# Zeroed pad columns, a later load and a new order for the head of a block kernel

## The chip, the cores and the metric

The kernel runs on one core of a Trainium2 chip. The metric is the device time of one execution in microseconds (us); a run gives several executions, and their median is compared. The engines of the core are TensorE (PE, with its weight loads PEld), VectorE (DVE), ScalarE (ACT), GpSimd (POOL) and SyncE (SP, which here issues DMAs).

## The reference

One token block with adaptive layer norm: the vector c makes six modulation rows, an attention with a sliding window of 256 follows (16 heads of 28), and then a gated MLP whose gate mixes along the sequence. x is 2048 x 448; everything is bfloat16.

```
mod = (silu(c) @ w_mod).reshape(1, 6, 1, 448)      # w_mod: 448 x 2688
sa, ca, ga, sb, cb, gb = the six rows of mod
h = layernorm(x) * (1 + ca) + sa
x = x + ga * attention(h, wqkv, wo)                # keys within 256 before the query
h = layernorm(x) * (1 + cb) + sb
z = gelu(h @ w_in); z1, z2 = halves of z; z2 = layernorm(z2)
x = x + gb * ((z1 * (w_sp @ z2 + b_sp)) @ w_out)
```

## The kernel before, in words

The kernel is written as a list of operations, each with its dependencies. The string ORDER fixes, in one sequence over all engines, in which order they run: a word such as `158.a` or `50.p.0` is the number of an operation, its engine (p PE, a ACT, v DVE, g POOL, s SP) and, where it takes a buffer, which one. Each engine runs its operations in this order and never out of order. `Sched.order` reads the string, `waits` puts a semaphore wait only where an operation's dependency isn't known to be done, `emit` writes the instructions. An operation that waits therefore holds everything behind it on its engine.

The sequence is cut into 16 tiles of 128 rows and four blocks of 512. The work around the change is that of the first block, in the first 20 us:

- Loads, all on SP in this order: x of tiles 0 to 3 (ops 1, 2), the first 896 columns of w_mod in four row chunks kc (ops 4 to 7, `t_wmA`), the q and k columns of wqkv in chunks (ops 8 to 10; chunk 3 is op 3 on ACT's queue), wv (11, 12), x of tiles 4 to 7 (13), the other 1792 columns of w_mod (14, 15, `t_wmB`), x of tiles 8 to 11 (16).
- c is turned into a column by PE (op 41) and put through silu by ACT in two pieces (ops 42 and 43, `t_sc`). DVE zeroes the padding rows of the fourth chunk of w_mod (23, `t_p2`) and of c's column (22, 25).
- The statistics of tiles 0 to 3: bn_stats and bn_aggr on DVE (L581, L584), the reciprocal root on POOL (L586, L587), xn on DVE (L594), transposes on PE (L625; ops 150, 152, 154, 156).
- The modulation of the first norm: for each chunk kc PE makes eight columns of 128 (L537 to L541; ops 50 to 53, `t_mA`), and DVE adds up the four chunks into modT (op 54, L543). D is 448, so the last of the eight columns holds only 64; before the change it is first written with zeros by a product with the zero tile wz and then its lower half with a product of 64 columns.
- hT: the transposed xn leaves PSUM with scale and shift from modT, one operation for each of four channels ch (ops 157 to 160, in the order ch 3, 0, 1, 2; L635 on ACT, L636 on DVE). Each waits for op 54 and for all four transposes.
- WQK: the q and k weights of each chunk are copied from wq_st into a padded layout (ops 133 to 136; L573 on ACT, L574 on DVE or POOL).
- PE then makes q and k of the block, eight groups of four products (L646), evicted to qT and KT (L654 on ACT, L655 on DVE). Attention starts on those (L855, L881, L842).
- Fillers (L549) are products on wz whose result nobody reads.
- The rows for ga, gb, sb, cb come from a later product of PE with the other columns of w_mod (op 119, `t_rows`, L556), which needs sc_rep (op 48, L531), a copy of c's column repeated 32 times.
- Ops 44 to 47 zero the tile QBD, 27 the padding of wv, 36 writes ones into Vaug, 38 and 39 build the mask.

After the first 20 us the order is the same in both kernels.

Of the kernel before, what the change touches and what calls it, by code (L numbers as in the profile page):

```python
# [23 lines left out]
191.p.0 178.p 163.p 44.g 173.p 179.p 166.p.2 180.a 186.p.1 167.p 174.p 182.p 217.v 175.a 168.p 169.p 215.v 164.p 170.a 187.p 192.p 219.v 188.p 165.a  # L24
189.p 213.v 183.p 190.a 374.p.0 216.v 220.v 184.p 214.v 218.v 375.a.0 193.p 221.g 185.v 196.p.1 222.g 194.p 197.p 195.v 198.p 199.p 201.p.6 225.g
200.v 210.s 227.g 226.g.0 17.s 202.a 380.p.0 228.v.1 381.a.1 223.g 212.s 229.g 224.v.2 119.p.0 30.g 18.s 230.v.3 376.v 211.s 231.p.1 120.a 399.p.0
232.v 121.s 234.p.0 400.a.2 233.v 209.s 203.p.6 235.v 19.s 401.a 205.p.1 236.v 123.s 265.v 204.a 406.p.0 206.v 239.p.0 407.a.3 267.v 378.v 251.p.1
# [239 lines left out]
def bass_adaLN_cond__sliding_block__mixer_gmlp__prompt_kernel(  # L267
# [56 lines left out]
    sc_sb, _, _ = alloc("sc_sb", [128, DC], BF16)  # L324
# [31 lines left out]
    wmod, _, wmod_bytes = alloc("wmod", [128, DC, 6 * D], BF16, at=z2_off)  # L356
# [69 lines left out]
    t_wmA = [chunk("d_wmA", "sp", wmod, w_mod, kc, slice(0, 2 * D), -98.95 + 0.001 * kc, LAND_M[kc], 0.23) for kc in range(DC)]  # L426
# [12 lines left out]
    t_wmB = load2("d_wmB", "sp", 1.4, wmod, slice(2 * D, 6 * D), w_mod, slice(2 * D, 6 * D), (), -94.0)  # L439
# [13 lines left out]
    def pool(dur, fn, deps=(), prio=-90.0):  # L453
        return add({"pool": (dur, fn)}, deps, prio)
# [37 lines left out]
    t_p2 = [dve(1.2, lambda e: e.memset(wmod[64:128, 3, :], 0.0), prio=-98.0)]  # L492
# [29 lines left out]
    t_sc = [  # L522
        act(0.25, lambda e: e.activation(sc_sb[:, 0:3], ps[:, hC.slot[0], 0:3], ACT.Silu), [t_cT, t_p1], -90.0, table="silu"),
        act(0.25, lambda e: e.activation(sc_sb[0:64, 3:4], ps[0:64, hC.slot[0], 3:4], ACT.Silu), [t_cT, t_p1], -90.0, table="silu"),
    ]
# [7 lines left out]
    t_wz = dve(0.08, lambda e: e.memset(wz[:], 0.0), prio=-99.9)  # L533
    hA = Hold(bM)
    t_mA = []
    for kc in range(DC):
        fs = [lambda e, v=v, ch=ch, kc=kc, n=n: e.matmul(  # L537
            ps[:, hA.slot[0], 8 * kc + n:8 * kc + n + 1], lhsT=wmod[:, kc, v * D + ch * 128:v * D + ch * 128 + 128], rhs=sc_sb[:, kc:kc + 1],
            start=True, stop=True) for n, (v, ch) in enumerate((v, ch) for v in (0, 1) for ch in range(DC))][:7]
        fs += [lambda e, kc=kc: e.matmul(ps[:, hA.slot[0], 8 * kc + 7:8 * kc + 8], lhsT=wz[:], rhs=wz[:, 0:1], start=True, stop=True),  # L540
               lambda e, kc=kc: e.matmul(ps[0:64, hA.slot[0], 8 * kc + 7:8 * kc + 8], lhsT=wmod[:, kc, 2 * D - 64:2 * D], rhs=sc_sb[:, kc:kc + 1], start=True, stop=True)]  # L541
        t_mA.append(pe(0.23, fs, [t_wmA[kc], t_sc, t_p2, t_wz] + t_mA[-1:], -60.0 + 0.1 * kc, [] if kc else [hA]))
    t_modA = [dve(0.16, lambda e: e.tensor_reduce(modT[:, 0:8], ps[:, hA.slot[0], 0:32].rearrange("p (k n) -> p n k", k=4), mybir.AxisListType.X, ALU.add), [t_mA], -59.0)]  # L543
    hA.until += t_modA

    def warm(n, dur, times, cols):
# [11 lines left out]
        start=(kc == 0), stop=(kc == DC - 1), tile_position=(0, 32 * i)) for kc in range(DC) for i, v in enumerate((2, 5, 3, 4))],  # L558
# [127 lines left out]
    for tb in range(1, NB4):  # L686
        v = 40.0 * tb - 50.0
# [24 lines left out]
        for cp in range(0 if tb >= PET else 2):  # L712
# [6 lines left out]
            for k in range(2):  # L719
                ch = 2 * cp + k  # L720
# [353 lines left out]
    for tb in range(NB4):  # L1074
# [16 lines left out]
        for i in range(4):  # L1091
# [102 lines left out]
```

## Time and profile before

| | |
|---|---|
| median of 3 runs | 277.41 us (276.78 to 278.3) |
| profiled execution, its own time | 278.0 us |
| its span in the profile | 276.3 us, 7324 instructions |
| busy PE, PEld | 265.5 (96%), 140.1 (51%) |
| busy DVE, ACT, POOL | 163.4 (59%), 128.5 (47%), 116.8 (42%) |
| largest groups | L1079 PE 97.9 us, L842 ACT 67.2 us, L897 DVE 37.6 us |

The span is the time from the first to the last instruction; the execution's own time has 1.7 us around it. Matmuls are pipelined, so a PE that is busy 96% isn't at its peak. In the timeline a row gives start, length, engine, line, operation, what it writes and reads, a count where rows were merged, and in brackets how long the engine was idle before it and what ended that. In the chain of waits a row gives start, length and what held the chain. A DMA row gives size and time from issue to landing.

### The profile page before, as it was taken

The numbers are of one execution on the slowest core, as the hardware profiler recorded it, in microseconds if no ns is written. First come the engines' busy times: TensorE is split into PE (matmuls) and PEld (weight loads), VectorE is DVE, ScalarE is ACT, GpSimd is POOL, SyncE is SP. The second block draws the span as 40 slices with busy tenths as digits, with TensorE's granted clock in tenths as the row PEclk, the third lists the DMA queues.
The fourth block names the chain that finished last, engine by engine and source line by source line (L and its number), as shares of the span: only waits on it lengthen the run. The fifth ranks groups of instructions, "written<-read, shape, count | busy, mean of one in ns | idle before, by whom it ended". The sixth has DMA issues, their size and how long they took to land.

```text
span 276.3 us, 7324 instructions
## 1 busy us (share of the span) xinstructions
PE 265.5 (96%) x3176; PEld 140.1 (51%) x3201; DVE 163.4 (59%) x359; ACT 128.5 (47%) x152; POOL 116.8 (42%) x192
## 2 busy tenths in 40 slices
PE   7899998999999999999999999999999999999995
PEld 2545465656676575544444444444444444544452
DVE  7668999999999999666899210014021222331453
ACT  7589999989999996847766500000000000000000
POOL 5340856055334894896169110018033352541310
PEclk9999999999999999999999999999999999999999
DMA  7956244253763377668699989300000000010024
GB/s 217 359 149 166 56 78 81 59 96 77 227 89 80 62 111 157 98 133 134 131 164 187 189 194 191 75 0 0 0 0 2 0 0 2 0 33 17 19 67 133
DMA packets 66862, 26.48 MB, mean 96 GB/s; under 512 B 57801, under 2 KB 65742, under 8 KB 66830
## 3 DMA queue, kind: packets, MB, share of 16 engines
q1 hardware_dynamic: 66748, 25.90, 44.1%
q8 instruction: 25, 0.41, 0.7%
q10 hardware_dynamic: 82, 0.12, 0.1%
q14 instruction: 7, 0.06, 0.1%
HBM read 9.47 MB, written 1.84 MB: 41 GB/s over the span
## 4 chain that ended last, share of the span: by engine, by line
PE 75%; ACT 10%; DVE 8%; POOL 2%; issue 2%; DMA 2%
PE ps L1079 35%; PE ps L1096 7%; ACT PW L842 7%; PE ps L1055 6%; PE ps L1034 6%; PE ps L881 4%; PE ps L737 3%; PE ps L924 3%; DVE st_all L581 3%; PE ps L949 3%; PE ps L779 2%; PE ps L890 2%; DMA hT<-xn 2%; PE ps L766 1%; ACT PT L842 1%
## 5 line engine op out<-in xcount | busy, mean ns | idle before, releaser
L842 ACT ACTIVATE PW<-ps 128x2048 bf16<-128x2048 f32 (+1 forms) x56 | 67.2, 1240 | 4.4 <-PE ps L881 2.5
L1083 DVE TENSOR_TENSOR tmpg<-ps,bsp_bc 128x512 bf16<-128x512 f32 x28 | 18.9, 688 | 80.0 <-PE ps L1079 70.2
L1086 POOL TENSOR_TENSOR z1T<-tmpg,z1T 128x512 bf16<-128x512 bf16 x28 | 31.9, 1154 | 80.5 <-DVE tmpg L1083 80.5
L1079 PE MATMUL ps<-wspB,z 128*128 128x512 bf16 x219 | 49.2, 379 | 0.3
L1079 PE MATMUL ps<-wspA,z 128*128 128x512 bf16 x219 | 48.7, 379 | 0.4 <-issue 0.2
L897 DVE TENSOR_TENSOR PT<-PW,mask 128x1024 bf16<-128x1024 bf16 x56 | 37.6, 702 | 0.4 <-ACT PW L842 0.3
L1079 PEld LDWEIGHTS ps<-wspA,z 128*128 128x128 bf16 x224 | 21.8, 98 | 26.6 <-issue 0.4
L1079 PEld LDWEIGHTS ps<-wspB,z 128*128 128x128 bf16 x224 | 21.9, 98 | 26.1
L586 POOL TENSOR_SCALAR ve_all<-mv_all 128x1 f32<-128x1 f32 (+2 forms) x37 | 10.7, 299 | 53.0 <-DVE mv_all L584 52.6
L587 POOL TENSOR_TENSOR rs_all<-ve_all,neghalf 128x1 f32<-128x1 f32 (+2 forms) x37 | 26.2, 720 | 0.9
L924 PE MATMUL ps<-Vaug,PT 128*128 128x29 bf16 x496 | 24.6, 176 | 0.3 <-issue 0.3
L924 PEld LDWEIGHTS ps<-Vaug,PT 128*128 128x128 bf16 x496 | 22.1, 96 | 3.5 <-issue 0.8
L1034 PE MATMUL ps<-w_in,hT 64*128 64x448 bf16 x224 | 22.7, 349 | 0.3 <-POOL hT L974 0.3
L1055 PE MATMUL ps<-hT,w_in 64*128 64x512 bf16 x196 | 22.5, 376 | 0.0
L581 DVE BATCH_NORM_STATS2 st_all<-z 128x6 f32<-128x448 bf16 x32 | 17.9, 600 | 4.7 <-ACT z L1041 4.7
L924 PE MATMUL ps<-Vaug,PW 128*128 128x29 bf16 x224 | 20.6, 175 | 0.0
L1096 PE MATMUL ps<-w_out_g,z1T 128*128 128x448 bf16 x105 | 20.4, 352 | 0.0
L581 DVE BATCH_NORM_STATS2 st_all<-x_sb 128x6 f32<-128x448 bf16 x32 | 19.1, 612 | 0.1
L924 PEld LDWEIGHTS ps<-Vaug,PW 128*128 128x128 bf16 x224 | 17.7, 96 | 2.4
L737 PE MATMUL ps<-hT,WQK 128*128 128x512 bf16 x66 | 17.2, 379 | 1.6 <-issue 0.5
L1041 ACT ACTIVATE z<-ps 128x896 bf16<-128x896 f32 x16 | 14.2, 916 | 8.4 <-PE ps L1034 8.4
L1063 ACT ACTIVATE z1T<-ps 128x512 bf16<-128x512 f32 x28 | 15.0, 610 | 6.2 <-PE ps L1055 6.2
(117 smaller groups left out, 332.7 us busy)
## 6 DMA issues: line engine op xcount, KB each, us to landing
out_dram<-fin SPq DMA_DIRECT2D x15, 112.0 KB, 1.7
x_sb<-in_A_x_dram SPq DMA_DIRECT2D x3, 448.0 KB, 5.6
wmod<-in_w_mod_dram SPq DMA_DIRECT2D x1, 1344.0 KB, 9.2
w_in<-in_B_w_in_dram SPq DMA_DIRECT2D x1, 1344.0 KB, 6.1
QBD<-qT SPq DMA_DIRECT2D x16, 64.0 KB, 2.4
wmod<-in_w_mod_dram SPq DMA_DIRECT2D x4, 224.0 KB, 4.3
w_out_g<-in_B_w_out_dram SPq DMA_DIRECT2D x1, 784.0 KB, 6.3
wq_st<-in_A_wqkv_dram SPq DMA_DIRECT2D x3, 224.0 KB, 4.4
```

Source lines behind the costliest of these rows:

```text
L581: st = [dve(0.62 if True else 0, lambda e, t=t, ci=ci, s=s: e.bn_stats(st_all[:, slot, t, ci, :], s()), deps(t), prio) for ci, s in enumer ...
L587: rs = pool(0.53 + 0.15 * len(tiles), lambda e: e.tensor_tensor(rs_all[:, slot, a:b], ve_all[:, slot, a:b], neghalf[:, 0:b - a], ALU.pow), ...
L737: m = pe(4 * MMS, [lambda e, h=h, g=g, kc=kc, tb=tb: e.matmul(ps[:, h.slot[0], :], lhsT=WQK[:, kc, 4 * g:4 * g + 4, :].rearrange("p a b -> ...
L842: ex = act(xdur, lambda e, out_ap=out_ap, in_ap=in_ap: e.activation(out_ap(), in_ap(), ACT.Exp, scale=SCALE), [s], v - 8.0 + u, takes, tab ...
L897: return dve(0.70, lambda e: e.tensor_tensor(cols(hp.slot[0] * 2048 + 1024 * k, [[256, 4], [128, 2], [1, 128]]), cols(at_w() + 128 + 192 * ...
L924: fns.append(lambda e, hp=hp, hO=hO, hi=hi, bi=bi, kb=kb, hd=hd, nb=nb, a=at[hi][bi], p_of=p_of: e.matmul(ps[:, hO.slot[0], 32 * hd:32 * h ...
L1034: return lambda e, kc, p0, start, stop: e.matmul(ps[:, hs[t % 2].slot[hf], 0:D], lhsT=hT[p0:p0 + 64, kc, t * 128:(t + 1) * 128], rhs=w_in[ ...
L1055: return lambda e, kc, p0, start, stop: e.matmul(ps[:, hs[b // 2].slot[b % 2], :], lhsT=w_in[p0:p0 + 64, kc, ft * 128:(ft + 1) * 128], rhs ...
L1079: m = pe(16 * MMS, [lambda e, h=h, si=si, ft=ft, tb=tb: e.matmul(ps[:, h.slot[0], :], lhsT=z2[:, si, ft * 128:(ft + 1) * 128], rhs=(wspA i ...
L1083: a = dve(0.7, lambda e, h=h, ht=ht, tb=tb: e.tensor_tensor(tmpg[:, ht.slot[0], :], ps[:, h.slot[0], :], bsp_bc[:, tb * 512:(tb + 1) * 512 ...
L1086: u = pool(1.16, lambda e, ht=ht, ft=ft, tb=tb: e.tensor_tensor(z1T[tb][:, ft, :], tmpg[:, ht.slot[0], :], z1T[tb][:, ft, :], ALU.mult), [ ...
L1096: return [lambda e, ft=ft: e.matmul(ps[:, h.slot[0], 0:D], lhsT=z1T[t // 4][:, ft, (t % 4) * 128:(t % 4 + 1) * 128], rhs=w_out_g[:, ft, :] ...
```

## The change

- A new operation (1227, `t_pad`) on POOL zeroes columns 896 to 959 of w_mod in SBUF. The eighth column of products then reads 128 columns like the others, the last 64 of them zeros, so the two special products L540 and L541 are gone. Every group of products waits for the pad.
- Those columns belong to the second load of w_mod, so both of its transfers (`t_wmB`) now wait for all four groups of products.
- The head of ORDER is new: op 25 goes ahead of the aggregates, 43 ahead of the QBD zeroing 46, product groups 50 and 51 ahead of the first transposes; 48 and 27 go from right behind op 54 to behind the hT evictions; 158 moves from ACT to DVE, 133 from DVE to ACT; 159 comes before 160; 39 goes behind the second statistics on POOL. SP's order stays.

The head of ORDER (the rest of the string is only wrapped differently):

```diff
-49.v 20.v 1.s 31.g 0.a 3.a 47.a 21.v 23.v 2.s 4.s 32.g 24.v 40.a 5.s 6.s 33.g 37.g 7.s 139.v 34.g 35.g 29.g 55.p.0 56.p.0 57.p.0 41.p.0 38.g 137.v 8.s
-22.v 140.v 138.v 9.s 143.v 141.g 39.g 10.s 25.v 142.g 145.v 42.a 46.a 11.s 144.v 146.v 149.v.0 12.s 147.g 151.v.1 43.a 58.p.0 59.p.0 60.p.0 61.p.0
-62.p.0 63.p.0 64.p.0 65.p.0 66.p.0 67.p.0 150.p.1.2 148.g 26.v 13.s 50.p.0 152.p 14.s 153.v.2 68.p.0 51.p 155.v.3 69.p.0 52.p 15.s 154.p 53.p 16.s
-156.p 136.a 54.v 48.v 27.v 157.v 158.a 133.v 70.p.0 71.p.0 72.p.0 176.p.3 36.v 161.p.4 160.v 134.a 162.p 171.p.5 159.v 181.p.6 172.p 135.g 177.p 45.a
+49.v 20.v 1.s 31.g 0.a 3.a 47.a 21.v 23.v 2.s 4.s 32.g 24.v 40.a 5.s 6.s 33.g 37.g 7.s 139.v 34.g 35.g 1227.g 29.g 55.p.0 56.p.0 57.p.0 41.p.0 38.g
+137.v 8.s 22.v 25.v 140.v 138.v 9.s 143.v 141.g 10.s 142.g 145.v 42.a 43.a 46.a 11.s 144.v 146.v 149.v.0 12.s 147.g 151.v.1 58.p.0 59.p.0 60.p.0
+61.p.0 62.p.0 63.p.0 64.p.0 65.p.0 66.p.0 67.p.0 50.p.0 51.p 150.p.1.2 148.g 39.g 26.v 13.s 152.p 153.v.2 68.p.0 155.v.3 69.p.0 52.p 154.p 53.p 14.s
+15.s 16.s 156.p 136.a 133.a 54.v 157.v 158.v 70.p.0 71.p.0 72.p.0 176.p.3 36.v 161.p.4 159.v 160.v 134.a 162.p 171.p.5 48.v 27.v 181.p.6 172.p 135.g
```

```diff
     for kc in range(DC):
         fs = [lambda e, v=v, ch=ch, kc=kc, n=n: e.matmul(
             ps[:, hA.slot[0], 8 * kc + n:8 * kc + n + 1], lhsT=wmod[:, kc, v * D + ch * 128:v * D + ch * 128 + 128], rhs=sc_sb[:, kc:kc + 1],
-            start=True, stop=True) for n, (v, ch) in enumerate((v, ch) for v in (0, 1) for ch in range(DC))][:7]
-        fs += [lambda e, kc=kc: e.matmul(ps[:, hA.slot[0], 8 * kc + 7:8 * kc + 8], lhsT=wz[:], rhs=wz[:, 0:1], start=True, stop=True),
-               lambda e, kc=kc: e.matmul(ps[0:64, hA.slot[0], 8 * kc + 7:8 * kc + 8], lhsT=wmod[:, kc, 2 * D - 64:2 * D], rhs=sc_sb[:, kc:kc + 1], start=True, stop=True)]
-        t_mA.append(pe(0.23, fs, [t_wmA[kc], t_sc, t_p2, t_wz] + t_mA[-1:], -60.0 + 0.1 * kc, [] if kc else [hA]))
+            start=True, stop=True) for n, (v, ch) in enumerate((v, ch) for v in (0, 1) for ch in range(DC))]
+        t_mA.append(pe(0.37, fs, [t_wmA[kc], t_sc, t_p2] + t_mA[-1:], -60.0 + 0.1 * kc, [] if kc else [hA]))
...
+    t_pad = pool(0.35, lambda e: e.memset(wmod[:, :, 2 * D:2 * D + 64], 0.0), t_p2[0:1], prio=-97.0)
+    for op in t_mA:
+        op.deps.add(t_pad)
+    for op in t_wmB:
+        op.deps.update(t_mA)
+
     sc.order()
```

More of the change, by code (lines that the diff above doesn't have):

```diff
@@ L24 @@
[L24 to L27, printed above, removed]
@@ new lines @@
+201.p.6 225.g 200.v 210.s 227.g 226.g.0 17.s 202.a 380.p.0 228.v.1 381.a.1 223.g 212.s 229.g 224.v.2 119.p.0 30.g 18.s 230.v.3 376.v 211.s 231.p.1
+120.a 399.p.0 232.v 121.s 234.p.0 400.a.2 233.v 209.s 203.p.6 235.v 19.s 401.a 205.p.1 236.v 123.s 265.v 204.a 406.p.0 206.v 239.p.0 407.a.3 267.v
+378.v 251.p.1 266.v 269.v 408.a 271.v 428.p.0 377.p.0 240.a 379.p 268.v 272.v 426.p.0 270.v 252.v 273.g 243.p.0 274.g 427.a.4.0 402.v 384.v 382.v
+237.p.1 279.g 244.v 280.g.0 383.p 238.v 429.a 434.p.0 275.g 285.s 409.v 247.p.0 435.a.5.1 28.v 325.v 128.g 241.p.1 248.v 321.v 281.g 457.p.0 277.g
@@ new lines @@
+306.v 466.a 126.g 291.p.1 514.a.3.1 461.p.0 468.v 339.s 295.p.0 467.v 292.a 330.v.3 462.p 517.v 296.a 521.p.0 488.v 486.p.0 522.a.4.2 303.p.1 489.v
+469.p 496.v 389.p.0 304.a 526.v 470.p 487.a 542.p.0 471.v 472.v.1 297.p.1 543.a.5.3 390.v 473.s 494.p.0 497.v 490.p.0 491.p 391.v 498.p 337.s 495.a
+518.v 550.p.0 298.v 499.p 551.a.6.4 445.p.0 500.v 340.s 501.v.0 416.p.1 446.v 525.v 515.p.0 338.s 571.p.0 516.a 546.v 293.p.0 572.a.0.0 447.v 392.v
+519.p.0 417.v 393.g 520.p 394.g 502.s 554.v 523.p.0 301.p.1 524.a 395.g 294.v 396.v.0 579.p.0 124.s 302.a 576.v 299.p.0 307.s 580.a.1.1 343.g 418.v
@@ new lines @@
+310.s 448.v 474.p.1 555.v 308.s 344.g 419.v 552.p.0 475.v 527.p 300.a 309.s 528.p 341.g 553.a 600.p.0 529.v 530.v.2 420.g 317.p.1 449.g 601.a.2.2
+397.g 584.v 531.s 503.p.0 450.g 583.v 544.p.0 451.g 547.v 548.p.0 398.s 545.a 608.p.0 342.v 318.a 504.v 573.p.0 549.p 476.v 574.a 556.p 557.p
+609.a.3.3 575.v 345.p.1 477.v 558.v 559.v.1 581.p.0 311.p.0 605.v 560.s 346.a 505.v 629.p.0 582.a 604.v 577.p.0 630.a.4.4 130.s 349.p.1 452.v.1 612.v
+578.p 350.v 610.p.0 585.p 611.a 634.v 637.p.0 312.v 586.p 638.a.5.0 602.p.0 613.v 315.p.1 313.p.0 316.v 603.a 506.v 587.v 658.p.0 507.g 588.v.0 421.g
@@ new lines @@
+660.p.0 659.a.6.1 532.p.1 453.v 478.g 633.v 454.s 508.g 606.p.0 533.v 607.p 479.g 614.p 641.v 589.s 314.a 666.p.0 480.g 661.a 422.g 481.v.2 615.p
+509.g 667.a.0.2 534.v 347.p.1 482.g 483.s 616.v 535.v 617.v.2 561.p.0 423.v.0 631.p.0 424.g 618.s 562.v 536.g 687.p.0 632.a 510.g.1 348.v 635.p.0
+688.a.1.3 357.p.0 662.v 563.v 636.p 425.s 639.p.0 642.v 361.p.1 640.a 670.v 358.a 643.p 132.s 663.v 362.a 695.p.0 671.v 668.p.0 696.a.2.4 644.p 692.v
+351.p.0 645.v 646.v.1 590.p.1 691.v 647.s 669.a 716.p.0 564.v 352.a 591.v 565.g 664.p.0 511.g 717.a.3.0 699.v 665.p 353.s 672.p 566.g 839.v 697.p.0
```

32 lines of the change are left out of this document (10 added, 22 removed).

## The prediction

> **What bounds the kernel now.** I read the page first, then the chain of waits, then the timeline of the first 21 us engine by engine, and last the landings of single transfers.
>
> ```profile
> span 276.3 us, 7324 instructions
> ...
> 10.96 0.54 DVE hT L636
> ...
> 11.82 0.76 issue
> ...
> 13.69 2.56 PE ps L646 x11
> 16.28 0.60 ACT KT L654
> ```
>
> The first row is the page's, the others are from the chain of waits (start, length, what). In the head the chain lies on VectorE (DVE), which turns three of the four channels of hT out of PSUM; only at 13.69 does TensorE (PE) take it over, and then ACT with the evictions. Whatever starts the hT evictions earlier starts the rest earlier.
>
> ```profile
> 5.64 0.06 DVE L494 MEMSET sc_sb<- 1x1 bf16 x1
> 5.73 0.63 DVE L581 BATCH_NORM_STATS2 st_all<-x_sb 128x6 f32<-128x448 bf16 x1
> 7.78 0.70 DVE L594 TENSOR_SCALAR xn<-x_sb,mv_all,rs_all 128x448 bf16<-128x448 bf16 x2
> 9.75 0.19 DVE L543 TENSOR_REDUCE modT<-ps 128x8 f32<-128x32 f32 x1 [1.26 <-PE ps L541]
> 9.86 0.72 DVE L531 COPY sc_rep<-sc_sb 128x128 bf16<-128x128 bf16 x1
> 10.96 0.54 DVE L636 TENSOR_SCALAR hT<-ps,modT 128x512 bf16<-128x512 bf16 x1
> 13.55 2.19 DVE L581 BATCH_NORM_STATS2 st_all<-x_sb 128x6 f32<-128x448 bf16 x4
> ...
> 5.74 0.17 ACT L523 ACTIVATE sc_sb<-ps 128x3 bf16<-128x3 f32 x1
> 5.81 1.05 ACT L528 ACTIVATE QBD<-zero 128x1024 f32<-128x1024 f32 x1
> 6.75 0.15 ACT L524 ACTIVATE sc_sb<-ps 64x1 bf16<-64x1 f32 x1
> 7.78 0.95 ACT L573 ACTIVATE WQK<-wq_st 128x896 bf16<-128x896 bf16 x1 [0.87 <-DVE wq_st L495]
> 10.14 0.78 ACT L635 ACTIVATE hT<-ps,modT 128x512 bf16<-128x512 bf16 x1 [1.41 <-PE ps L625]
> ...
> 6.92 0.40 PE L625 MATMUL ps<-ident,xn 128*128 128x128 bf16 x4 [0.63 <-DVE xn L594]
> 7.15 0.32 PE L537 MATMUL ps<-sc_sb,wmod 128*128 128x1 bf16 x7
> 9.25 0.32 PE L537 MATMUL ps<-sc_sb,wmod 128*128 128x1 bf16 x7
> 9.52 0.19 PE L541 MATMUL ps<-sc_sb,wmod 128*64 128x1 bf16 x1
> 9.64 0.40 PE L625 MATMUL ps<-ident,xn 128*128 128x128 bf16 x4
> 9.88 0.81 PE L549 MATMUL ps<-wz 128*128 128x512 bf16 x3
> 11.79 1.67 PE L646 MATMUL ps<-hT,WQK 128*128 128x512 bf16 x7 [1.10 <-ACT WQK L573]
> 13.69 3.84 PE L646 MATMUL ps<-hT,WQK 128*128 128x512 bf16 x17 [0.23 <-DVE hT L636]
> ```
>
> These are the timelines of DVE, ACT and PE. Four groups of products (L537 to L541, one for each chunk kc of w_mod) make the modulation; the reduction at 9.75 collects them, and every hT eviction waits for it. The reduction waited for PE (1.26). PE began its first group at 7.15, because the silu of c was complete only at 6.75 + 0.15 = 6.90: a zeroing of QBD stands on ACT between its two halves. Behind the reduction DVE first does sc_rep (0.72) and the zeroing of wv, which nobody needs yet, and evicts at 10.96. PE does fillers on wz until 10.69 and then waits.
>
> **The change, part by part.** All times are in this profiled execution: 278.0 us, 1.7 more than its span, and 0.6 above the median 277.41 of the runs.
>
> *The silu.* L524 now follows L523 at once and ends at 5.74 + 0.17 + about 0.1 = 6.0 instead of 6.90. The QBD zeroing behind it then lasts to about 7.05, in front of an ACT idle until 7.78: nothing. So the first two groups can run at 6.1 and at 6.35, ahead of the first transposes (L625), which waited for xn anyway.
>
> *The products.* In the last group the first product starts at 9.25 and the last ends at 9.71; in place of L540 and L541 comes one more product like the other seven. Seven take 0.32 of which 0.16 is the latency of one, so a step is 0.025 and eight end after 0.34: 0.12 less on the path, 0.16 less of issue in each group.
>
> *The statistics.* The memset L494 at 5.64 moves ahead of the aggregates. The two stats rows around it started 0.77 apart, and four in a row (13.55, 2.19 with the last one's 0.61) start 0.53 apart: up to 0.24 is saved, but the memset now costs some 0.1 in front of the first of them. I take 0.12 (bounds 0 and 0.24). The mask selection that stood on POOL between two statistics moves behind them and takes nothing away from the path. The xn of tiles 2 and 3 thus come at 7.66 instead of 7.78; the first of them (0.39) is ready at 8.1.
>
> *PE up to the reduction.* Behind both early groups come transposes 0 and 1 (from 6.8), two fillers (0.22 each), group 2 by 7.95, transpose 2 at 8.11 when xn is there, group 3 at 8.33, its end at 8.67, and transpose 3 at 8.55 to 8.93. The reduction starts at 8.75 instead of 9.75. The pieces of w_mod that these groups read are there:
>
> ```profile
> wmod<-in_w_mod_dram SPq DMA_DIRECT2D x1, 112.0 KB, 4.6
> 3.25 0.59 SPq L418 DMA_DIRECT2D wmod<-in_w_mod_dram  x1
> ```
>
> The last was issued at 3.25 and landed 4.6 later, at 7.85, before 8.33.
>
> *Behind the reduction.* The first eviction follows directly: it starts when reduction and last transpose are done, at 9.0 instead of 10.96. That is 1.0 for the earlier reduction and 0.96 for sc_rep and the wv zeroing moved away. The second channel goes from ACT to DVE (9.5 to 10.05), the WQK piece of L574 from DVE to ACT, idle between 8.7 and 10.14 (0.95, to about 9.55), and ACT's next WQK piece follows, to 10.5. PE's first two products start at 9.6, the third at 10.1, then one each 0.216 (17 in 3.84). The ninth, which waits for the third hT channel, started at 13.69; now PE reaches it at 10.1 + 6 x 0.216 = 11.4. The channel is ready at about 10.9 if DVE runs through, and at about 11.65 if the 0.76 of "issue" at 11.82, which nothing in the profile explains, appears again. So the head gains 2.3 or 2.05.
>
> A rule and its row:
>
> ```profile
> 9.57 0.93 POOL L574 COPY WQK<-wq_st 128x896 bf16<-128x896 bf16 x1 [1.82 <-DMA wq_st<-in_A_wqkv_dram]
> 10.44 1.03 POOL L529 MEMSET QBD<- 128x1024 f32 x1
> ```
>
> The three transfers of wq that stand behind w_mod's on SP landed between 7.85 and 9.5, where POOL's copy of the last one was released; the first at the latest at about 9.0, and the copy on ACT would then end at 9.95, still ahead of the second channel. POOL works from 9.57 to 11.47, over all of DVE's new evictions. Before, sc_rep took 0.72 for 128 elements and ended at 10.58, just behind POOL's copy (10.50), as if held by it; the eviction at 10.96 took its plain 0.54 in the middle of POOL's memset and was not held. The Trainium skill, "SBUF — State Buffer", section "Who interferes with whom", has DVE in a 2-port mode and GpSimd exclude each other for whole instructions, tensor_scalar among the candidates. If that held for the evictions, the third would start behind POOL's copy at 10.5 and the fourth behind its memset at 11.47, and the gain would be about 2.1 instead of 2.3; the row at 10.96 speaks against it.
>
> *The pad.* One memset more on POOL, 4 x 64 elements in each partition:
>
> ```profile
> 2.42 0.31 POOL L498 MEMSET xn<- 128x256 bf16 x1
> 5.09 0.24 POOL L586 TENSOR_SCALAR ve_all<-mv_all 128x2 f32<-128x2 f32 x1 [2.11 <-DVE mv_all L584]
> ```
>
> The same size took 0.31, and POOL then idles 2.11: nothing. Without that cover it would put 0.31 on the statistics. The removed L540/L541 are counted above.
>
> *The late loads.* wmod's other columns now wait on SP for the last group, so they are issued at about 8.75 instead of 7.09; queued behind them on SP is the load of x for tiles 8 to 11, and then only the spreading of qT, which waits for evictions that come later still.
>
> ```profile
> 7.09 0.51 SPq L408 DMA_DIRECT2D wmod<-in_w_mod_dram  x1
> wmod<-in_w_mod_dram SPq DMA_DIRECT2D x1, 1344.0 KB, 9.2
> 6.46 0.59 SPq L413 DMA_DIRECT2D x_sb<-in_A_x_dram  x1
> x_sb<-in_A_x_dram SPq DMA_DIRECT2D x1, 448.0 KB, 5.6
> 20.57 0.94 PE L556 MATMUL ps<-wmod,sc_rep 128*32 128x448 bf16 x16
> ```
>
> The x load issued in front landed at 6.46 + 5.6 = 12.06, the w_mod load at 7.09 + 9.2 = 16.29, and its small last part, issued 0.55 behind it, I take at about 17. Its reader L556 ran at 20.57, and after the shift would at 18.3. One end: the transfers stand in line behind x's until 12.06 and land when they did, 1.3 before use. The other end: they take their 9.2 from the issue again and land at 17.95, the last part at about 18.7, and PE waits 0.4. I take the first, as x's transfer was still landing 3 us after the new issue; the second stays in the range.
>
> *What then is late.*
>
> ```profile
> 19.41 0.69 DVE L655 CAST KT<-ps 128x512 bf16<-128x512 f32 x1
> 21.44 0.62 PE L714 MATMUL ps<-ident,xn 128*128 128x128 bf16 x8
> ```
>
> From 16.28 on ACT's evictions and exponentials follow PE back to back, so they move with it. DVE's moved sc_rep and wv zeroing put the statistics of the next block (13.55) at 12.4, a gain of only 1.15; xn of that block is read by the transposes at 21.44, and DVE made it only behind its evictions, which ended at 20.1, so some slack covers the difference; how much no row here tells, and I take it as about enough. Sum: 2.1, between 2.05 and 2.3. Profiled 275.9, median 277.41 - 2.1 = 275.3.
>
> **The rivals.**
>
> *Only half arrives.* The next block's statistics (gain 1.15) take the lead, or the late w_mod lands at its far end: 1.2 instead of 2.1, so 276.2. For it speaks that this slack is not wide; against it, that DVE's evictions stand between the two in any case.
>
> *The head moves and the end does not.* A later stage waits for something not tied to the head: 277.4. The chain from 13.69 on knows only PE, ACT, DVE, POOL and transfers which these issue, and L1079 with its neighbours is PE without a gap; little speaks for it.
>
> *Slower: PE loses its clock.*
>
> ```profile
> 1.04 1.46 PE L549 MATMUL ps<-wz 128*128 128x512 bf16 x3 [1.04 <-DVE one L491]
> 2.74 3.55 PE L549 MATMUL ps<-wz 128*128 128x512 bf16 x10
> ```
>
> At the start three fillers took 1.46, 0.42 apart; at 9.88 they are 0.215 apart. Ten from 2.74 took 3.55 where the fast step would give 2.3, so about six of them were slow and the step changed at about 5, some 4 us after the first. If PE between 6.1 and 9.6, with more waits and fewer fillers in between, fell back to the slow step for another 4 us, about 10 to 17 of the 32 products at 0.216 more each would cost 2.2 to 3.7: net 0.1 to 1.6 slower, about 278.3. It decides by the idle stretch: the fillers before outlived stretches of 0.63 and 1.10, and the longest now is about 0.7. The Trainium skill, "TensorE: Matmul & The Clock Gate", Part 1, puts the fall behind an idle window of about 3.4 us; by that it does not happen.
>
> *The order does not do what it says:* a wait that I missed holds the early groups and only sc_rep's 0.96 stays: 276.4. This lies with the half gain.
>
> **How the numbers follow.** The full gain 0.68, half 0.16, none 0.09, slower 0.07. About 0.5%, 1.4 us, is what can be told from no change here. The full gain is above it nearly always, the half one in about half of its cases: faster 0.76, same 0.16, slower 0.08. The runs before span 276.78 to 278.3, so 0.6 of scatter at least is in the median. Range: low 275.3 - 0.3 (the gain at 2.3, with 0.1 for the aggregates) - 0.6 = 274.4; high 277.2, which takes in half gains with scatter and most of none.
>
> **What would show it.** The reduction near 8.75, the first hT eviction near 9.0, L646 without the gap at 13.69, KT L654 at 12.4 to 12.7 instead of 14.77, L556 near 18.3 without a wait on wmod. Wrong: L556 waiting for wmod, the statistics on DVE in the chain, or L549/L646 products 0.42 apart.

## The result and the profile after

| kernel | median of its runs | ratio to before, 95% interval | profiled execution, span |
|---|---|---|---|
| before | 278.08 us (276.76 to 279.88, 20 runs) | | 278.0, 276.3 |
| changed | 275.78 us (274.7 to 277.32, 20 runs) | 0.9927 [0.9908, 0.9945] | 275.76, 274.0 |

The changed kernel is 2.3 us faster; forecast was 2.1. The size was right, but the head that brought it isn't the one that was forecast. First the span from the page, then rows of the chain of waits of the changed kernel:

```profile
span 274.0 us, 7317 instructions
...
2.31 5.73 DMA wmod<-in_w_mod_dram
8.44 0.47 PE ps L623 x8
...
10.30 0.55 DVE hT L634
11.13 4.18 PE ps L644 x18
...
19.69 0.87 PE ps L554 x16
```

Two things are new. The pieces of DVE and the "issue" that stood in the chain between 10.96 and 13.69 are gone: from 11.13 PE runs 18 products in one stretch (L644, before L646). But in front of it the chain no longer starts at PE's own order; it hangs on a load, the second row chunk of w_mod, issued at 2.31 and landed 5.73 later.

The timelines of DVE and ACT in the changed kernel:

```profile
9.98 0.19 DVE L541 TENSOR_REDUCE modT<-ps 128x8 f32<-128x32 f32 x1 [1.57 <-PE ps L537]
10.30 1.00 DVE L634 TENSOR_SCALAR hT<-ps,modT 128x512 bf16<-128x512 bf16 x2
12.07 0.63 DVE L634 TENSOR_SCALAR hT<-ps,modT 128x512 bf16<-128x512 bf16 x1 [0.77 <-DVE hT L634]
12.17 0.27 DVE L506 MEMSET Vaug<- 128x256 bf16 x1
13.05 0.22 DVE L531 COPY sc_rep<-sc_sb 128x128 bf16<-128x128 bf16 x1
...
5.73 0.15 ACT L524 ACTIVATE sc_sb<-ps 64x1 bf16<-64x1 f32 x1
13.82 0.60 ACT L652 ACTIVATE KT<-ps 128x512 bf16<-128x512 f32 x1 [1.46 <-PE ps L644]
```

The reduction is at 9.98, which is later than before (9.75), not earlier. The first eviction to KT is at 13.82 instead of 14.77, and all of that was won behind the reduction: the first hT eviction stands 0.32 behind the reduction instead of 1.21. The row of before for KT:

```profile
14.77 0.60 ACT L654 ACTIVATE KT<-ps 128x512 bf16<-128x512 f32 x1 [2.07 <-PE ps L646]
```

PE's timeline in the changed kernel shows why the reduction was late:

```profile
7.50 0.35 PE L537 MATMUL ps<-sc_sb,wmod 128*128 128x1 bf16 x8 [0.92 <-DMA wmod<-in_w_mod_dram]
8.09 0.35 PE L537 MATMUL ps<-sc_sb,wmod 128*128 128x1 bf16 x8 [0.24 <-DMA wmod<-in_w_mod_dram]
8.30 0.61 PE L623 MATMUL ps<-ident,xn 128*128 128x128 bf16 x8
...
9.18 0.34 PE L537 MATMUL ps<-sc_sb,wmod 128*128 128x1 bf16 x8
...
9.60 0.34 PE L537 MATMUL ps<-sc_sb,wmod 128*128 128x1 bf16 x8
...
19.62 0.94 PE L554 MATMUL ps<-wmod,sc_rep 128*32 128x448 bf16 x16
```

The silu was done at 5.88, but PE waited 0.92 for the first row chunk of w_mod and 0.24 for the second; the transposes (L623), fillers and the other two groups follow in PE's queue without a wait. From the second group to the reduction it is here 1.89 of PE's own work.

### The profile page after: what moved, and what is told of

Its sections match the earlier page's. It is cut to its first block, busy times and chain, and to the rows that moved or that the text cites. A ratio compares the mean times of both kernels' runs of the same rounds, so it can differ in the third digit from the quotient of the medians.

```text
span 274.0 us, 7317 instructions
## 1 busy us (share of the span) xinstructions
PE 264.9 (97%) x3172; PEld 139.5 (51%) x3197; DVE 162.4 (59%) x359; ACT 128.5 (47%) x152; POOL 117.1 (43%) x193
## 4 chain that ended last, share of the span: by engine, by line
PE 76%; ACT 13%; DVE 5%; DMA 2%; POOL 1%; issue 1%; SPq 1%; DVEq 0%
PE ps L1077 35%; ACT PW L840 9%; PE ps L1094 7%; PE ps L1053 6%; PE ps L1032 6%; PE ps L879 4%; PE ps L735 3%; PE ps L922 3%; PE ps L947 3%; DMA wmod<-in_w_mod_dram 2%; PE ps L777 2%; DVE st_all L579 2%; PE ps L888 2%; PE ps L644 2%; PE ps L764 1%
## 5 line engine op out<-in xcount | busy, mean ns | idle before, releaser
L1081 DVE TENSOR_TENSOR tmpg<-ps,bsp_bc 128x512 bf16<-128x512 f32 x28 | 18.8, 688 | 80.0 <-PE ps L1077 70.2
L579 DVE BATCH_NORM_STATS2 st_all<-z 128x6 f32<-128x448 bf16 x32 | 17.9, 602 | 4.7 <-ACT z L1039 4.7
```

The source lines that it names most:

```text
L579: st = [dve(0.62 if True else 0, lambda e, t=t, ci=ci, s=s: e.bn_stats(st_all[:, slot, t, ci, :], s()), deps(t), prio) for ci, s in enumer ...
L1081: a = dve(0.7, lambda e, h=h, ht=ht, tb=tb: e.tensor_tensor(tmpg[:, ht.slot[0], :], ps[:, h.slot[0], :], bsp_bc[:, tb * 512:(tb + 1) * 512 ...
```

## The experiments

Ratios are to the kernel before, run on the same chip in turn with the others. Line numbers are of each kernel itself: those built from the changed kernel have its numbers, the others those of before. In the diffs "..." in ORDER stands for words left as they are.

**The changed kernel again.** No edit.

> The changed kernel once more, unchanged. In its first profile w_mod's first 896 columns landed 1.2 to 1.6 us later than in the profile of before, the modulation's reduction started at 9.98 and the first eviction to KT at 13.82. Theory A (that lateness is chance): here w_mod lands by 7.9 to 8.3, the reduction starts at 8.7 to 9.0, the first hT eviction at 9.0 to 9.2, the first KT eviction at 12.4 to 12.7. Theory B (the change itself makes w_mod land late): the last piece of w_mod lands at 9.0 or later again. Time by both: 0.990 to 0.995 of before.

> The changed kernel once more, unchanged, beside the other: ratio 0.991 to 0.993. Theory of the landings: the reduction comes 0.4 to 0.8 behind the last landing of w_mod, wherever that falls between 8.2 and 9.3, and the first eviction 0.3 behind the reduction.

Measured: 275.68 us, ratio 0.991 [0.9888, 0.9933], and 275.87 us, 0.9937 [0.9917, 0.9957]. Rows of the second one's PE, DVE and ACT:

```profile
7.11 0.35 PE L537 MATMUL ps<-sc_sb,wmod 128*128 128x1 bf16 x8 [0.49 <-DMA wmod<-in_w_mod_dram]
...
18.64 0.94 PE L554 MATMUL ps<-wmod,sc_rep 128*32 128x448 bf16 x16
19.52 0.62 PE L712 MATMUL ps<-ident,xn 128*128 128x128 bf16 x8
...
9.00 0.19 DVE L541 TENSOR_REDUCE modT<-ps 128x8 f32<-128x32 f32 x1 [0.60 <-PE ps L537]
9.33 1.00 DVE L634 TENSOR_SCALAR hT<-ps,modT 128x512 bf16<-128x512 bf16 x2
...
12.85 0.60 ACT L652 ACTIVATE KT<-ps 128x512 bf16<-128x512 f32 x1 [1.34 <-PE ps L644]
```

The same instructions came 0.98 earlier, because the chunk did. The reduction is again 1.89 behind the second group, the first eviction 0.33 behind the reduction, KT 3.85 behind it (3.84 in the first profile). So in these two profiles one landing, that of the second chunk, moves the whole head. That the reduction follows the last landing by 0.4 to 0.8, as expected, holds in size (0.68), but the rows correct the mechanism: PE waits for the second chunk and is then busy for longer than the other two need.

The first repeat fits neither of its two theories: the last chunk landed at 8.73, between them, the reduction came at 9.18 and KT at 13.02, later than the theory of chance had it. There the second group waited for its chunk and the third, at 8.37, for its own, so the reduction stood 1.93 behind the second group. And the chain of that profile hangs on yet another load, a chunk of wq, whose copy into WQK on ACT was done 0.03 behind the first hT eviction:

```profile
3.89 5.21 DMA wq_st<-in_A_wqkv_dram
9.12 0.96 ACT WQK L571
...
10.33 4.18 PE ps L644 x18
```

These are the landings of the four row chunks of w_mod (issued at about 1.80, 2.31, 2.78 and 3.25 in all kernels), read from the traces, with what followed:

```
kernel                       chunk 0  1     2     3     2nd group  reduction  1st hT eviction  KT
before                       5.73  6.32  7.44  7.84     8.00       9.75       10.96            14.77
DVE's order alone            6.09  6.95  7.78  8.37     7.92       9.68       10.09            13.68
ones on GpSimd, before       6.04  7.14  7.77  8.31     7.92       9.67       10.38            14.51
early products alone         6.74  7.46  8.09  8.62     7.50       9.93       10.63            15.41
pad and late load alone      6.82  7.66  8.37  8.92     7.71       9.36       10.07            13.88
new order alone              6.08  7.01  7.95  8.37     7.05       9.48        9.89            13.48
changed                      7.45  8.04  8.65  9.23     8.09       9.98       10.30            13.82
changed, again               6.19  7.20  8.32  8.73     7.25       9.18        9.50            13.02
changed, again (2)           6.22  7.06  7.78  8.32     7.11       9.00        9.33            12.85
changed, sc_rep back         6.40  7.52  8.20  8.65     7.57       9.46       10.16            13.68
still earlier head           6.26  7.21  7.81  8.28     7.58       9.07       9.30             12.72
rows moved                   6.42  7.26  8.14  8.69     7.58       9.22       9.45             12.87
```

The landing differs by up to 1.7 between executions that issue it at the same time. The profile of before caught the earliest of all, that of the changed kernel the latest. Whether that is chance alone isn't shown: the last chunk landed at 8.28 to 9.23 in the seven profiles with the pad and at 7.84 to 8.62 in the five without, so the ranges overlap, but some tenths of lateness by the change itself aren't excluded. In the old order with the special products it hardly matters, for the landings seen there: the second group stands at about 8.0 behind transposes and fillers, and the reduction at 9.67 to 9.75. With products 50 and 51 ahead of the transposes the second group starts 0.05 behind its chunk.

**DVE's order alone**, on the kernel before:

```diff
-136.a 54.v 48.v 27.v 157.v 158.a 133.v ... 160.v 134.a 162.p 171.p.5 159.v 181.p.6
+136.a 133.a 54.v 157.v 158.v ... 159.v 160.v 134.a 162.p 171.p.5 48.v 27.v 181.p.6
```

> Before, with the new order on DVE and ACT behind the reduction alone (sc_rep and the zeroing of wv behind the hT evictions, second channel on DVE, WQK chunk 0 on ACT). My theory (two separate gains, about 1 us each): the reduction stays at 9.75, the first hT eviction follows at 10.1 instead of 10.96, KT at 13.6 to 13.9 instead of 14.77; 0.9 to 1.2 us faster, ratio 0.996. Rival 1 (DVE's order is the whole gain, as the first profile of the changed kernel looks): ratio 0.992 to 0.993. Rival 2 (the late loads are the gain): ratio 1.000.

Measured: 276.78 us, 0.9948 [0.9929, 0.9967]. The reduction stays (9.68), the first eviction comes at 10.09 and KT at 13.68: 1.09 earlier, as expected and as the step "Behind the reduction" said. By its median it is the largest of the three parts, though its interval overlaps that of the pad below.

**Early silu and products alone**, on the kernel before:

```diff
-22.v 140.v ... 141.g 39.g 10.s 25.v 142.g ... 42.a 46.a ... 43.a 58.p.0 ... 67.p.0 150.p.1.2 148.g ... 50.p.0 152.p ... 51.p 155.v.3
+22.v 25.v 140.v ... 141.g 10.s 142.g ... 42.a 43.a 46.a ... 58.p.0 ... 67.p.0 50.p.0 51.p 150.p.1.2 148.g 39.g ... 152.p ... 155.v.3
```

> Before, with the earlier silu, the two early product groups and the earlier memset alone; special products, early loads and the order on DVE behind the reduction stay. My theory: the reduction starts at 8.9 to 9.1 instead of 9.75, the first hT eviction at 9.6 to 10.2, 0.7 to 1.3 us faster, ratio 0.995 to 0.997. Rival 1 (DVE's order is the whole gain): ratio 0.999 to 1.001. Rival 2 (late loads): 1.000.

Measured: 277.8 us, 0.9978 [0.9957, 1.0]. In its profile the second group waited for its chunk, with the transposes queued behind it, and the reduction came at 9.93, not at 8.9 to 9.1 as expected. Then, from the timelines of DVE, POOL and ACT:

```profile
11.09 1.36 DVE L574 COPY WQK<-wq_st 128x896 bf16<-128x896 bf16 x1
13.22 0.62 DVE L636 TENSOR_SCALAR hT<-ps,modT 128x512 bf16<-128x512 bf16 x1 [0.77 <-DVE WQK L574]
...
10.38 0.93 POOL L574 COPY WQK<-wq_st 128x896 bf16<-128x896 bf16 x1 [2.46 <-DMA wq_st<-in_A_wqkv_dram]
11.26 0.95 POOL L529 MEMSET QBD<- 128x1024 f32 x1
...
15.41 0.60 ACT L654 ACTIVATE KT<-ps 128x512 bf16<-128x512 f32 x1 [2.54 <-PE ps L646]
```

DVE's copy of a WQK chunk took 1.36 and ended at 12.45, behind POOL's memset (12.21). KT came 0.64 later than before. Alone, the earlier products gain next to nothing. Here the landing kept the reduction late and the copy held up the evictions; that the earlier products pay once the copy has left DVE is argued from this, not shown by this run.

**Pad, plain products and late load alone**, in before's order (the code of the changed kernel, with 1227 behind 35 and ops 14 to 16 behind 53):

```diff
-34.g 35.g 29.g ... 13.s 50.p.0 152.p 14.s ... 52.p 15.s 154.p 53.p 16.s 156.p
+34.g 35.g 1227.g 29.g ... 13.s 50.p.0 152.p ... 52.p 154.p 53.p 14.s 15.s 16.s 156.p
```

> Before, with the pad on POOL, eight plain products in each group and the loads behind the products alone; the old order stays. My theory: PE runs from 7.1 on without a gap up to the reduction, four groups are 0.16 shorter each, so the reduction starts at 9.1 to 9.3, 0.4 to 0.6 us faster, ratio 0.998. Rival 1: ratio 1.000. Rival 2 (the late loads are the gain): ratio 0.992 to 0.993 and wq lands earlier than 9.51.

Measured: 276.96 us, 0.9959 [0.9941, 0.9977]. The reduction came at 9.36, some 0.3 to 0.4 earlier than in the kernels of the old order with the special products, and a little later than the 9.1 to 9.3 expected: in this execution the chunks landed late, and the third and fourth groups, too, started 0.05 behind theirs (8.37 and 8.92). DVE's WQK copy was quick:

```profile
8.41 0.35 PE L537 MATMUL ps<-sc_sb,wmod 128*128 128x1 bf16 x8
...
8.97 0.35 PE L537 MATMUL ps<-sc_sb,wmod 128*128 128x1 bf16 x8
...
10.53 0.39 DVE L572 COPY WQK<-wq_st 128x896 bf16<-128x896 bf16 x1
```

It had begun when POOL began its copy, at 10.67, since that chunk of wq had landed only at 10.61; this time it was POOL's copy that took longer, 1.03 for 0.93. So part of KT's 13.88 is a collision missed, by the landing of this execution; the other part is the products. The median gained 1.0, more than the 0.3 to 0.4 of the products, and one profile doesn't tell where the remainder lies. The three parts give 0.52, 0.41 and 0.22%, together 1.15%, and the whole change 0.6 to 0.9%: within the intervals they add up.

**The new order alone**: special products, no pad, w_mod's other columns loaded early. The code is that of before; the diff of ORDER is against the changed kernel, and 1227 is left out as well.

```diff
-67.p.0 50.p.0 51.p 150.p.1.2 148.g 39.g 26.v 13.s 152.p 153.v.2 68.p.0 155.v.3 69.p.0 52.p 154.p 53.p 14.s 15.s 16.s 156.p
+67.p.0 50.p.0 51.p 150.p.1.2 148.g 39.g 26.v 13.s 14.s 15.s 16.s 152.p 153.v.2 68.p.0 155.v.3 69.p.0 52.p 154.p 53.p 156.p
```

> The whole new order, but with the special products L540 and L541 and without the pad, the late columns of w_mod loaded early as before. My theory now (order is worth most; the shorter products are worth something because the reduction follows the landing of w_mod's last piece; the late load is worth nothing and costs nothing): the reduction starts 0.7 to 0.9 behind the landing of the last piece instead of 0.45 in the second profile of the changed kernel, the late columns land at 16.6 to 18.1 and nobody waits for them; ratio 0.992 to 0.994. Rival 1 (the late load is part of the gain): ratio 0.996 or more. Rival 2 (the late load is a cost, since its landing at 18.76 came 0.06 before its use): ratio 0.989 to 0.990.

Measured: 276.02 us, 0.9947 [0.9922, 0.9972]. From the second group to the reduction it takes 2.43 here (7.05 to 9.48), 1.89 in the changed kernel: the plain products save 0.54 over three groups. The reduction stood 1.11 behind the last landing, more than the 0.7 to 0.9 expected. That the late load brought anything isn't seen: here the early columns landed at 17.15 and 17.97, and w_mod's first chunks no later than in the kernels that load late.

**sc_rep and wv's zeroing back** behind the reduction, in the changed kernel:

```diff
-54.v 157.v 158.v ... 171.p.5 48.v 27.v 181.p.6
+54.v 48.v 27.v 157.v 158.v ... 171.p.5 181.p.6
```

> The changed kernel with sc_rep and the zeroing of wv put back between the reduction and the hT evictions, where they were. My theory: the first eviction comes 0.7 behind the reduction (0.22 for sc_rep, 0.1, 0.25 for the memset) instead of 0.33, or 1.0 to 1.2 where POOL's copy of WQK holds sc_rep as in the profile of before; ratio 0.9925 to 0.995. Rival (DVE's order was the whole gain): ratio 0.998 to 1.000.

Measured: 275.87 us, 0.993 [0.9906, 0.9954], no difference that these runs can show. sc_rep took 0.22 where it had taken 0.72 in before, and the first eviction came 0.70 behind the reduction, so KT was 13.68 with the chunk at 7.52. The 0.96 of the prediction was the price in one execution; here the move is worth 0.37.

**Vaug's ones on GpSimd**, on the kernel before. The 0.77 in front of the third eviction is the same, 0.76 to 0.78, in every profile in which DVE writes these ones:

```diff
-    t_va = [dve(0.36, lambda e: e.memset(Vaug[:, :, :, DH:DH + 1], 1.0), prio=-98.5)]
+    t_va = [pool(0.36, lambda e: e.memset(Vaug[:, :, :, DH:DH + 1], 1.0), prio=-98.5)]
-... 38.g 137.v ... 176.p.3 36.v 161.p.4
+... 38.g 36.g 137.v ... 176.p.3 161.p.4
```

> Before, with the ones of Vaug written by POOL at about 3.0 instead of by DVE between two hT evictions. Theory A (the stall of 0.77 which every profile so far has in front of that memset belongs to the memset): no stall, the third eviction follows the second copy on DVE at once, KT at 14.3 to 14.5 where WQK's copy on DVE is not held by POOL, ratio 0.998 to 0.999; POOL shows the same work as a longer or later row. Theory B (it belongs to the place, the eviction waits for something in PSUM): the 0.77 stays in front of the next eviction, ratio 1.000.

Measured: 277.49 us, 0.9983 [0.9963, 1.0004]. DVE and POOL:

```profile
9.78 0.22 DVE L531 COPY sc_rep<-sc_sb 128x128 bf16<-128x128 bf16 x1
...
10.84 1.25 DVE L574 COPY WQK<-wq_st 128x896 bf16<-128x896 bf16 x1
12.01 0.98 DVE L636 TENSOR_SCALAR hT<-ps,modT 128x512 bf16<-128x512 bf16 x2
...
2.92 1.23 POOL L506 MEMSET Vaug<- 128x256 bf16 x1
10.02 0.93 POOL L574 COPY WQK<-wq_st 128x896 bf16<-128x896 bf16 x1 [2.34 <-DMA wq_st<-in_A_wqkv_dram]
10.89 0.95 POOL L529 MEMSET QBD<- 128x1024 f32 x1
```

The stall is gone, so the "issue" of the prediction is this memset: its row on DVE showed only 0.27, and 0.77 of it lay ahead of the row. On POOL, where it costs nothing, the whole row is 1.23. DVE's copy is held again (1.25), so KT gains only 0.26 on the profile of before. In the changed kernel even that is covered: KT stands 3.52 behind the first eviction with the stall, 3.42 without it (next kernel).

**A still earlier head.** The changed kernel with Vaug's ones on POOL, all groups of products behind the transposes that they held up, two fillers less, and only the 64 pad columns of w_mod loaded late (ops 1228, 1229):

```diff
-67.p.0 50.p.0 51.p 150.p.1.2 148.g 39.g 26.v 13.s 152.p 153.v.2 68.p.0 155.v.3 69.p.0 52.p 154.p 53.p 14.s 15.s 16.s 156.p
+67.p.0 150.p.1.2 148.g 39.g 26.v 13.s 14.s 15.s 152.p 50.p.0 51.p 52.p 153.v.2 155.v.3 154.p 156.p 53.p 1228.s 1229.s 16.s
-    t_wmB = load2("d_wmB", "sp", 1.4, wmod, slice(2 * D, 6 * D), ...
+    t_wmB = load2("d_wmB", "sp", 1.4, wmod, slice(2 * D + 64, 6 * D), ...
+    t_wmC = load2("d_wmC", "sp", 0.05, wmod, slice(2 * D, 2 * D + 64), w_mod, slice(2 * D, 2 * D + 64), t_mA, -94.0)
```

> The changed kernel with four more steps: ones of Vaug on POOL; all early transposes ahead of the products, the last group of products behind the last transpose and the two fillers between them left out; the late load split, so that only the 64 pad columns wait for the products and the other 1728 are loaded early. My theory: the reduction 0.4 behind the landing of w_mod's last piece and the first eviction 0.2 behind the reduction, evictions without a stall, late columns at 17 to 18; 0.2 to 0.5 us faster than the changed kernel, ratio 0.988 to 0.990. Rival (landings alone set the head and the rest is covered): as the changed kernel, 0.991.

Measured: 275.93 us, 0.9927 [0.9901, 0.9954]: the changed kernel's time. DVE, POOL, ACT and PE:

```profile
9.30 2.02 DVE L634 TENSOR_SCALAR hT<-ps,modT 128x512 bf16<-128x512 bf16 x4
11.24 0.89 DVE L531 COPY sc_rep<-sc_sb 128x128 bf16<-128x128 bf16 x1
...
10.22 0.93 POOL L572 COPY WQK<-wq_st 128x896 bf16<-128x896 bf16 x1 [2.30 <-DMA wq_st<-in_A_wqkv_dram]
11.10 0.95 POOL L529 MEMSET QBD<- 128x1024 f32 x1
...
12.72 0.60 ACT L652 ACTIVATE KT<-ps 128x512 bf16<-128x512 f32 x1 [1.28 <-PE ps L644]
...
19.40 0.94 PE L554 MATMUL ps<-wmod,sc_rep 128*32 128x448 bf16 x16 [0.82 <-DMA wmod<-in_w_mod_dram]
```

KT was the earliest of all, 2.05 ahead of before, but the product of the rows waited 0.82 for w_mod, whose last piece landed at 19.35 here. The bulk, issued at 7.12 almost as in before, landed at 18.49 and 19.04, not at 17 to 18 as expected; why isn't shown. At L554 the gain was down to 1.17 (19.40 for 20.57).

**The rows moved out of the way.** As the last, but with the changed kernel's late load unsplit, and the product of the rows some 2 us later and in another bank:

```diff
-    hR = Hold(bM)
+    hR = Hold(bH)
-... 119.p.0 30.g 18.s 230.v.3 376.v 211.s 231.p.1 120.a 399.p.0 232.v 121.s 234.p.0 ... 401.a
+... 30.g 18.s 230.v.3 376.v 211.s 231.p.1 399.p.0 232.v 234.p.0 119.p.0 ... 401.a 120.a 121.s
```

> The changed kernel with Vaug's ones on POOL, two fillers less, all product groups behind the transposes they used to hold up, and the product of the rows (L554) moved some 7 us later into another bank, so that the late columns of w_mod have time to land. Theory (the earlier version of this lost at L554 what it had won at KT): reduction 0.3 to 0.45 behind the last landing of w_mod, KT at 12.6 to 13.0, L554 without a wait on w_mod, ratio to the kernel before 0.988 to 0.990, 0.3 to 0.7 us under the changed kernel. Rival (the end doesn't follow a head that is earlier than the changed kernel's, because the landings and the transposes of hT set it): ratio 0.991 to 0.993 as the changed kernel's.

Measured: 276.73 us, 0.9952 [0.9931, 0.9973], against 0.9937 for the changed kernel beside it: no gain where 0.3 to 0.7 us was expected. KT came at 12.87 and L554 had no wait for w_mod, as expected. DVE and PE show what took their place:

```profile
17.51 0.69 DVE L653 CAST KT<-ps 128x512 bf16<-128x512 f32 x1
18.12 0.39 DVE L592 TENSOR_SCALAR xn<-x_sb,mv_all,rs_all 128x448 bf16<-128x448 bf16 x1
18.68 0.82 DVE L592 TENSOR_SCALAR xn<-x_sb,mv_all,rs_all 128x448 bf16<-128x448 bf16 x2 [0.17 <-POOL ve_all L596]
...
19.55 0.62 PE L712 MATMUL ps<-ident,xn 128*128 128x128 bf16 x8 [0.82 <-DVE xn L592]
...
20.99 0.94 PE L554 MATMUL ps<-wmod,sc_rep 128*32 128x448 bf16 x16
```

The next block's transposes (L712) can't run before xn is there, and DVE makes xn behind its own evictions. In the changed kernel L554 ends right where L712 starts (18.64 and 19.52 in the second repeat): it fills a hole of PE of just that length. Moved, it left the hole empty and cost its 0.87 at 20.99. Neither of these two beats the changed kernel.

## Why the prediction came out right

*The silu.* Right: 5.88 for 6.0. One reading beside it wasn't: in before PE's first group at 7.15 stood behind the first transposes, which waited for xn until 6.92, so the earlier silu alone would have moved nothing; it was the new place of the groups that let it count. *The products.* Right: 0.12 in the last group and 0.16 in each of the two before it make 0.44; measured 0.54. *The statistics.* Taken as 0.12, they gave nothing that shows: the second pair of xn starts at 7.70 or 7.71 in the changed kernel's profiles, and just so in the three kernels that keep the memset's old place; only the profile of before has 7.78. *The pad.* It cost POOL nothing.

*PE up to the reduction.* This step failed. It put the groups at 6.1 and 6.35 and the reduction at 8.75, and asked only of the last chunk whether it was there, in one execution: 7.85, the luckiest that was seen. The early groups need the first two chunks, which were there at 6.19 to 7.45 and 7.06 to 8.04 in the changed kernel's three profiles. They gave reductions at 9.98, 9.18 and 9.00. Against 9.67 to 9.75, the term of 1.0 was about 0.5 to 0.75 in two profiles and below nothing in one. What the step called earlier groups became a wait for a load with the transposes queued behind it.

*Behind the reduction.* Right in its mechanism. From the reduction to KT it said 3.65 to 3.95; the profiles show 3.84 and 3.85. The 0.96 for sc_rep was a high price, from an execution in which POOL's copy held it. In executions with later landings sc_rep takes 0.22, but then DVE's WQK copy runs into POOL's copy and memset instead and takes 1.25 to 1.36 for 0.39. Moving that copy to ACT, which the prediction counted only as room for the second channel, removes this. So KT of the old order is late in both kinds of execution, at 14.77 in the one and, even with Vaug's ones on POOL, at 14.51 in the other, for two different reasons. The "issue" gap appeared again, as the lower of the two values assumed.

*The rule on the lock.* The row of before spoke against it for the evictions, and the later rows show where it holds: four evictions took 2.02 straight across POOL's copy and memset, 0.5 each as without them, while copies from SBUF to SBUF were held, sc_rep (0.89 and 0.96 under POOL's memset, 0.22 without) and WQK's (1.25, 1.36; 0.39 without). The Trainium skill, "SBUF — State Buffer", section "Who interferes with whom", has the two engines shut each other out for whole instructions when DVE runs in a 2-port mode; for the copies the traces agree, for evictions out of PSUM they show no such wait.

*The late loads.* The step took the near end and got the far one: forecast 16.29 and about 17 or, at the far end, 17.95 and 18.7; the timeline of SP and the landings of its transfers show

```profile
9.97 0.37 SPq L408 DMA_DIRECT2D wmod<-in_w_mod_dram  x1
10.38 0.50 SPq L409 DMA_DIRECT2D wmod<-in_w_mod_dram  x1
wmod<-in_w_mod_dram SPq DMA_DIRECT2D x1, 1344.0 KB, 7.9
wmod<-in_w_mod_dram SPq DMA_DIRECT2D x1, 224.0 KB, 8.4
```

that is 17.9 and 18.8; in the repeats 17.91 and 18.76, then 16.75 and 17.81. L554 ran at 19.62, 18.82 and 18.64 without a wait, once with 0.06 to spare. That the late load gained anything isn't seen, and it took most of the slack: in before the last piece was there 3.5 ahead of L556.

*What then is late.* "About enough" was right, and the last two kernels show how little more there is: behind an earlier head first w_mod is late, and then xn of the next block. By the chain the gain of KT reached L554 whole: from KT to L554 it is 5.80 before and 5.79 to 5.80 after.

*The rivals.* "Only half arrives" has its two causes, w_mod at its far end and the next block, both at the edge of acting. PE's clock did not fall: the granted clock was 1.00 over the span, and its products stayed about 0.22 apart (4.18 for 18 with the last one's latency), though PE had idled 0.92 ahead of the first group; with that short a stretch, the Trainium skill, "TensorE: Matmul & The Clock Gate", Part 1, which wants some 3.4 us of idling, has no fall either.

*The sum.* At KT the changed kernel's profiles are 0.95, 1.75 and 1.92 ahead of before's, for 2.05 to 2.3 forecast, while the whole time fell by 2.3, 2.3 and 1.8 in the three comparisons. In the first profile part of what was missing came back by 41.5 (1.58 ahead there), where before's chain stood on a transpose of hT by DMA:

```profile
37.35 4.15 DMA hT<-xn
```

The same transfer took 3.2 in the changed kernel and 4.6 in both repeats; over all kernels it took between 2.5 and 4.6, so this looks like chance. The profiles of single executions thus show 1.75 to 1.92 at KT with ordinary landings. Where the last few tenths of the 2.3 come from isn't settled, but an estimate can be worked out: "Early silu and products alone" has before's order behind the reduction, and KT came there 5.48 behind it, where the profile of before has 5.02, since DVE's WQK copy was held. An execution of before like that, with the reduction at 9.7, would have KT at about 15.2, and the changed kernel's 13.02 and 12.85 would be 2.2 to 2.3 ahead. No second profile of before is there to show it. That 2.1 came so near is in part luck, then: the reduction gained 0.5 to 0.75 for 1.0, and by this estimate the WQK copy's move, which the sum did not price, made up for it.

## What to carry to other kernels

A transfer's landing in one profile is one draw: before work is pulled ahead to meet it, ask for each piece that the pulled work reads, and count with a spread as large as several executions show. On an engine that runs in order, work pulled ahead of other work hands its wait to all that stands behind it. And in the last two kernels an earlier head was passed on only as far as the next load and the next block's statistics were early too, so look for the piece of work that fills a hole before moving it out.

## What the runs showed of the hardware

- A load of 224 KB issued at the same time landed between 5.73 and 7.45, with the same queue around it in the first microseconds. A transfer signals its landing in 16 parts, and it counts as landed with the last: in the changed kernel's trace 15 parts of the first chunk were there by 6.20 and the last at 7.45. One packet took 1.30 us there, at 4.87, where the others took up to about 0.8; that it was this packet which made the last part late isn't shown, as the second repeat had one of 1.31 at 3.84, on ACT's queue, and landed the chunk at 6.22.
- Writing 256 scattered elements in each partition (Vaug's ones) holds DVE up by about 0.8 us: the four hT evictions take 2.84 with it in their midst (changed kernel, 10.30 to 13.14) and 2.02 without. Its row shows 0.27; on POOL the row shows 1.23. A memset on POOL of the same count in runs of 64 takes 0.31.
- POOL's plain memset of SBUF holds DVE's copies just as its copy does: sc_rep, 0.22 alone, ended 0.08 behind POOL's copy in before and 0.08 behind POOL's memset in the last two kernels; WQK's copy, 0.39 alone, ended about 0.25 behind the memset in two kernels, though its row begins while POOL was still at its copy.
